# Moving the last 96 columns of w1 into a projection, packing 34-row products in pairs, and fixing the order of a fused attention and MLP kernel by a table

## The chip, the cores and the metric

One NeuronCore of one Trainium2 chip. The metric is the device time of one execution in microseconds. The engines are TensorE (PE), VectorE (DVE), ScalarE (ACT), GpSimd (POOL) and SyncE (SP), which issues the DMAs.

## The reference

One sequence of S = 2048 tokens, D = 512 channels, 32 heads of 16, a hidden width of F = 1376. Attention looks at 8 positions, two tokens apart.

```python
def _A_ref(x, wqkv, wo):              # attention
    qkv = (x @ wqkv) -> q, k, v per head
    idx = pos[:, None] - (arange(8) * 2)[None, :]
    logits = einsum("bhsd,bhswd->bhsw", q, k[idx]) * Dh ** -0.5   # masked where idx < 0
    o = einsum("bhsw,bhswd->bhsd", softmax(logits), v[idx])
    return o.reshape(B, S, D) @ wo
def _B_ref(x, w1, b1, w2, b2):        # MLP
    h = gelu(layernorm(x) @ w1 + b1)
    return h @ w2 + b2
xn = layernorm(x)
return x + _A_ref(xn, wqkv, wo) * silu(_B_ref(xn, w1, b1, w2, b2))
```

## The kernel before

Every product is made of three fp16 products: a number is split into a high and a low fp16 part, and high x high, high x low and low x high are added in PSUM. With D = 512 = 4 x 128 a tile of projections takes 3 x 4 = 12 matmuls.

Tokens are split by parity (c = 0, 1), since the attention steps two tokens at a time, and into 16 tiles of 128. Heads are split into four blocks (hb). This makes eight units u, one for each (c, hb). `qkv(c, hb, u)` multiplies the 8 token tiles of a parity with the 384 columns of q, k and v of the block (L746), scales them on the way out of PSUM (ACT L763, DVE L759) into a buffer `U`, and SP copies shifted rows within `U` (L771), so that a neighbour in time lies on the same partition. `attention(c, hb, u)` then works on DVE:

- four products of 2048 columns q x k (L805), each summed over the head by a reduction (L808);
- the softmax (L828 to L837, with the exponential on ACT at L831);
- four products of 2048 columns of weights, which lie in PSUM (`pl`), with v (L863);
- their sum over the window. The sum of the first two products is one addition of 2048 columns on POOL (L873), the sum of the last two one on DVE (L858); both are then halved by POOL additions of 1024 columns (L883). Each of these comes behind a copy of one element (`gate`, L882), which holds it back until a q x k product of the next unit has ended, so that it runs beside a reduction;
- the high part (ACT L846) and the low part (DVE L848) of the output `o`, then a DMA transpose.

The MLP runs between these in four chunks (ch) of 512 tokens and 11 blocks (f) of 128 hidden columns; the last block has 96. `mlp1(ch, f)` makes the hidden columns (L1016), ACT applies gelu and writes the high part (L1036), DVE writes the low part from PSUM (L1038). `mlp2(ch, f)` adds a block to the four output tiles `z` (L1052). The last block of mlp2 has 96 hidden rows and one for the bias: 97. Output products are L929 and L961; DVE (L993, L1000) and POOL (L997) join the gate and x, and SP stores.

In the head, weights are loaded in fp32, ACT sums their squares for a scale (L514 for wqkv, L421 for w1), and ACT and DVE split them into high and low parts (L536, L543; L482, L486). The first tiles of y are cast by ACT (L687) after a transpose on PE.

The order is made in Python when the program is built. `Plan.add` records each operation with what it reads and writes, a priority and a duration; `Plan.issue` repeatedly takes, from the operations whose predecessors are placed, the one that can start earliest by a model of the engines (of equal ones the one with the first priority), and writes the instructions in that order. Each engine runs its own instructions strictly in the order in which they were written.

Of the kernel before, what the change touches and what calls it, by code (L numbers as in the profile page):

```python
# [8 lines left out]
F32 = mybir.dt.float32  # L9
F16 = mybir.dt.float16  # L10
# [23 lines left out]
LASTPOOL = (0, 2, 4)  # L34

# [3 lines left out]
LAG = 2  # L39

# [28 lines left out]
BEFORE_W1 = (0, 1, 4, 5)  # L69

# [26 lines left out]
class Plan:  # L97
# [89 lines left out]
    def place(self, o, t):  # L187

        if o.eng == "sp":
            if not o.nbytes:  # L190
                return t
            self.free["sp"] = t + o.issue
            self.dma = max(self.dma, t + o.issue + 0.3)
            self.dma += o.nbytes / (o.rate if self.dma > SLOW else 265e3)
            end = self.dma + o.tail
            self.landed.append((end, o.nbytes))
            return end
# [24 lines left out]
    def issue(self):  # L222
# [5 lines left out]
        order = []  # L228
        while len(order) < len(self.ops):
            best = None  # L230
            for e, cand in engs.items():
# [95 lines left out]
def tile_mixer(ctx, tc, a_x, a_xt, a_wqkv, a_wo, b_w1, b_b1, b_w2, out):  # L327
# [34 lines left out]
    ident = sb.tile([P, P], F32, name="ident")  # L362
    make_identity(nc, ident)
    fours = sb.tile([P, 2 * P], BF16, name="fours")
    nc.vector.memset(fours, 4.0)
    mean1 = sb.tile([P, P], F32, name="mean1")
    nc.vector.memset(mean1, 1.0 / D)
    halves = sb.tile([P, 16], F32, name="halves")
# [3 lines left out]
    misc = sb.tile([P, 512], F32, name="misc")  # L372
    v0 = misc[64:65]


    wq = sb.tile([P, NHB, 2, KT, 384], F16, name="wq")
    w1 = sb.tile([P, 2, KT * F], F16, name="w1")
# [6 lines left out]
    b1T = sb.tile([P, NF], F32, name="b1T")  # L384
    hlast = sb.tile([P, 2, 512], F16, name="hlast")
# [7 lines left out]
    R_mx = Ring(sb, [P, 64], F32, 4, "mx")  # L393
    R_cs = Ring(sb, [P, NI], F32, 8, "cs")
# [72 lines left out]
    def low_pool(n, lo, get, s, hi, **k):  # L467
# [4 lines left out]
        pool(0.45 + n * 3.9e-3, fn, **k)  # L472
# [36 lines left out]
    def scale_q(hb):  # L509
        col = R_s.new()  # L510
        for k in range(0, KT, 2):
            def go(k=k):
                src = stq[hb]()[:, k * 384:(k + 2) * 384]
                nc.scalar.activation(wq[:, hb, 0, k:k + 2].bitcast(BF16),  # L514
# [11 lines left out]
    def prep_q(hb):  # L526
# [3 lines left out]
        for k in range(0, KT, st):  # L530
            n = st * 384
            dst = [wq[:, hb, t, k:k + st].rearrange("p k e -> p (k e)") for t in range(2)]
            src = lambda k=k, n=n: stq[hb]()[:, k * 384:k * 384 + n]
# [117 lines left out]
    def y0(i):  # L651
# [12 lines left out]
        elif Y_ENG[i] == "pool":  # L664
            pool(1.25, lambda: nc.gpsimd.tensor_scalar(x(), x(), mv0[:, q, 0:1], rb0[:, q:q + 1], op0=ALU.subtract,
# [54 lines left out]

    def qkv(c, hb, u):
# [13 lines left out]
        raw = pl.users([("xc", j) for j in FP]) if u == 1 else set()  # L735
        csk = {i: (cs, g) for g in parts for i in g} if u == 0 else {i: cs for i in range(NI)}
        for n, i in enumerate((IORD0, IORD1)[u] if u < 2 else IORD):
# [5 lines left out]
            def mm(n0=0, n1=12, y=y, o=o, b=b):  # L743
                for n in range(n0, n1):
                    (s, t), k = ((0, 0), (1, 0), (0, 1))[n // KT], n % KT
                    nc.tensor.matmul(b.t[:, 0:384], y[:, s, k, o:o + P], wq[:, hb, t, k],  # L746
# [5 lines left out]
            for n0, n1 in zip([0] + ends, ends):  # L752
                pe(n1 - n0, 384, lambda mm=mm, n0=n0, n1=n1: mm(n0, n1), [("yh" if n1 <= 4 else "y", c, i)] +
# [8 lines left out]
            else:  # L762
                act(384, lambda i=i, b=b: nc.scalar.activation(  # L763
                    U3[:, i:i + 31:15, :], b.t[:, 0:384].rearrange("p (t e) -> p t e", t=3),
                    AF.Identity, scale=cs.t[:, cp(i):cp(i) + 1]), **ev)

# [241 lines left out]
    def mlp1(ch, f):  # L1008
        M = P if f < NF - 1 else FL
# [15 lines left out]
        if f < NF - 1:  # L1025
            h = R_h.new()
            hi, lo = (lambda: h.t[:, 0]), (lambda: h.t[:, 1])
        else:
            h = ("hlast",)
            hi, lo = (lambda: hlast[:, 0]), (lambda: hlast[:, 1])  # L1030
        hk = (h, 0) if f < NF - 1 else ("hlast", 0)
# [9 lines left out]
        hq[f] = (hi, lo, M if f < NF - 1 else M + 1, h, hk)  # L1041

    def mlp2(ch, f):
        hi, lo, K, h, hk = hq.pop(f)
        for t in range(4):
# [3 lines left out]
            def mm(t=t, z=zt[t]):  # L1049
                hl = (hi(), lo())  # L1050
                for n, (s, w) in enumerate(((0, 0), (0, 1), (1, 0))):
                    nc.tensor.matmul(z.t, hl[s][0:K, t * P:(t + 1) * P], w2[0:K, w, f],  # L1052
                                     start=(f == 0 and n == 0), stop=(f == NF - 1 and n == 2))
            pe(3, 512, mm, [h, hk, w2key[f]] + ([("hrow",)] if f == NF - 1 else []), [zt[t]])
# [23 lines left out]
    def mlp(n):  # L1078
        for _ in range(n):
# [4 lines left out]
            if p < len(steps):  # L1084
# [20 lines left out]
    def zero_halo(b):  # L1105
# [7 lines left out]
          lambda: f32v(s1h.t, 1)[:, 0, 0:W1C[4] - W1C[3]]]  # L1113
    s1k = [[("s1a", n, 0)] for n in range(2)] + [[s1o], [s1h]]
    s2a, s2b = f32v(yT[2], 4), f32v(yT[3], 4)
    s2c = [R_f.new() for k in range(3)]
# [250 lines left out]
```

## Time and profile before

| what | value |
|---|---|
| median of 3 runs | 414.9 us (414.75 to 414.92) |
| the profiled execution's own time | 415.18 us |
| its span in the trace | 413.4 us |
| PE busy | 405.9 us (98%) |
| DVE busy | 379.5 us (92%) |
| ACT busy | 222.1 us (54%) |
| POOL busy | 120.3 us (29%) |
| granted clock | 0.999 |

The profile is of one execution; its times count from the start of the span. An engine can be busy nearly all the time without being the bound, and the chain that ended last says which one was followed back from the end. In the lists of groups a row gives line, engine, operation, out<-in, shape and count, then busy time and the mean in ns of one, then the idle time before.

### The profile page before, as it was taken

The page shows a single profiled execution, that of the slowest core. Times are in us where ns is not written, and L with a number is a line of the kernel's source. Part 1 is how long each engine was busy: PE and PEld are TensorE (multiplying, and loading weights), DVE is VectorE, ACT ScalarE, POOL GpSimd, SP SyncE. Part 2 cuts the span into 40 slices and gives each one's busy share as a digit, 9 for nine tenths or more (in the row PEclk, how much of TensorE's full clock was granted, in tenths as well). Part 3 has the DMA queues.
Part 4 walks back from the last instruction along what each step waited for, and adds up shares of the span by engine and source line. Part 5 has one row for each costly group of instructions (what it writes and reads, how often), then busy time and mean ns, then how long its engine had stood idle before and what let it go on. Part 6 is the DMA issues. An engine that isn't in the chain of part 4 may idle for free.

```text
span 413.4 us, 5554 instructions
## 1 busy us (share of the span) xinstructions
PE 405.9 (98%) x2083; PEld 206.6 (50%) x2083; DVE 379.5 (92%) x379; ACT 222.1 (54%) x353; POOL 120.3 (29%) x131
## 2 busy tenths in 40 slices
PE   8799999999999999999999999999999999999996
PEld 5555544445654455445544554455455544444443
DVE  4996989998999999989998999999999998999954
ACT  4699899994549655843384252225212393263500
POOL 3834002004380425042504330434033404520021
PEclk9999999999999999999999999999999999999999
DMA  8958717030045137720172034223604244007133
GB/s 281 397 112 258 235 61 230 0 128 1 1 142 152 28 93 183 149 46 2 48 221 75 0 102 116 68 86 88 205 7 122 88 111 145 0 18 238 23 102 131
DMA packets 47211, 46.41 MB, mean 112 GB/s; under 512 B 31785, under 2 KB 32225, under 8 KB 46673
## 3 DMA queue, kind: packets, MB, share of 16 engines
q1 hardware_dynamic: 47184, 46.06, 37.6%
q8 instruction: 16, 0.26, 0.3%
q14 instruction: 11, 0.08, 0.1%
HBM read 24.06 MB, written 7.34 MB: 76 GB/s over the span
## 4 chain that ended last, share of the span: by engine, by line
PE 92%; ACT 3%; issue 1%; DVE 1%; POOL 1%; ACTq 0%
PE z L1052 28%; PE ps L1016 28%; PE ps L746 25%; PE ps L929 5%; PE ps L961 2%; PE z L961 2%; PE pl L746 1%; ACT w L421 1%; PE pl L961 1%; ACT f L673 1%; ACT yT L687 0%; ACT wq L536 0%; POOL wq L471 0%; POOL rb L635 0%; ACT prod L661 0%
## 5 line engine op out<-in xcount | busy, mean ns | idle before, releaser
L1016 PE MATMUL ps<-yT,w 128*128 128x512 f16 (+1 forms) x528 | 120.4, 379 | 0.0
L746 PE MATMUL ps<-wq,yT 128*128 128x384 f16 x708 | 117.0, 326 | 0.2 <-DVE U L759 0.2
L1052 PE MATMUL z<-w,h 128*128 128x512 f16 x480 | 110.4, 379 | 0.0
L746 PEld LDWEIGHTS <-yT 128*128 128x128 f16 x744 | 72.5, 98 | 49.2 <-issue 1.0
L1016 PEld LDWEIGHTS <-w 128*128 128x128 f16 (+1 forms) x528 | 52.8, 100 | 61.0
L805 DVE TENSOR_TENSOR prod<-U 128x2048 f32<-128x2048 f32 x32 | 73.2, 2286 | 2.2 <-POOL prod L883 0.7
L1052 PEld LDWEIGHTS <-h 128*128 128x128 f16 x480 | 46.6, 98 | 55.5 <-issue 0.3
L808 DVE TENSOR_REDUCE L<-prod 128x128 f32<-128x2048 f32 x32 | 73.0, 2281 | 0.4
L1033 ACT ACTIVATE ps<-ps,b1T,hsc 128x512 f32<-128x512 f32 (+1 forms) x44 | 32.9, 748 | 73.4 <-PE ps L1016 72.2
L863 DVE TENSOR_TENSOR prod<-pl,U 128x2048 f32<-128x2048 f32 x28 | 63.2, 2283 | 4.2 <-POOL prod L873 4.1
L763 ACT ACTIVATE U<-ps,cs 128x384 f32<-128x384 f32 x54 | 31.2, 580 | 65.2 <-PE ps L746 65.2
L873 POOL TENSOR_TENSOR prod<-prod,prod 128x2048 f32<-128x2048 f32 x7 | 31.7, 4531 | 113.8 <-DVE prod L863 99.6
L883 POOL TENSOR_TENSOR prod<-prod 128x1024 f32<-128x1024 f32 x14 | 32.9, 2349 | 0.0
L882 POOL COPY gate<-prod 1x1 f32<-1x1 f32 x21 | 5.5, 264 | 91.0 <-DVE prod L805 82.2
L1038 DVE SCALAR_TENSOR_TENSOR h<-ps,hsc,h 128x512 f16<-128x512 f32 x40 | 29.6, 741 | 1.7 <-ACT h L1036 1.4
L1036 ACT ACTIVATE h<-ps,hsc 128x512 f16<-128x512 f32 x40 | 27.3, 684 | 1.3 <-PE z L1052 0.4
L929 PE MATMUL ps<-wo,oT 128*128 128x512 f16 x96 | 21.7, 379 | 0.0
L858 DVE TENSOR_TENSOR prod<-prod,prod 128x2048 f32<-128x2048 f32 x9 | 20.5, 2282 | 0.0
L1033 ACT ACT_TABLE_LOAD x10 | 12.8, 1283 | 8.6 <-PE ps L1016 8.5
L883 POOL TENSOR_TENSOR prod<-prod,prod 128x1024 f32<-128x1024 f32 x7 | 16.4, 2347 | 0.0
L961 PEld LDWEIGHTS <-oT 128*128 128x128 f16 x108 | 10.6, 98 | 10.4
L929 PEld LDWEIGHTS <-oT 128*128 128x128 f16 x96 | 9.4, 98 | 11.2
(179 smaller groups left out, 377.8 us busy)
## 6 DMA issues: line engine op xcount, KB each, us to landing
f<-in_A_x_dram SPq DMA_DIRECT2D x31, 256.0 KB, 3.5
U<-U SPq DMA_DIRECT2D x16, 392.0 KB, 4.0
gd<-f SPq DMA_DIRECT2D x12, 256.0 KB, 3.4
prod<-in_A_x_dram SPq DMA_DIRECT2D x8, 256.0 KB, 6.9
oT<-in_B_w_dram SPq DMA_DIRECT2D x2, 1024.0 KB
yT<-in_B_w_dram SPq DMA_DIRECT2D x2, 1024.0 KB, 7.9
f<-gd SPq DMA_DIRECT2D x8, 256.0 KB, 2.7
out_dram<-f SPq DMA_DIRECT2D x8, 256.0 KB, 2.8
```

Source lines behind the costliest of these rows:

```text
L746: nc.tensor.matmul(b.t[:, 0:384], y[:, s, k, o:o + P], wq[:, hb, t, k], start=(n == 0), stop=(n == 11))
L763: act(384, lambda i=i, b=b: nc.scalar.activation(U3[:, i:i + 31:15, :], b.t[:, 0:384].rearrange("p (t e) -> p t e", t=3), AF.Identity, sca ...
L805: dve(2048, lambda p2=p2, g=g: nc.vector.tensor_tensor(p2(), q, slots(Ut, KH, 2 * g), op=ALU.mult), qk + [("kh", ub, 0), ("kh", ub, 1), (" ...
L808: dve(2048, lambda pr=pr, g=g: nc.vector.tensor_reduce(L3()[:, 2 * g:2 * g + 2], pr.t.rearrange("p (r f d) -> p r f d", r=2, d=DH), AX.X, ...
L863: dve(2048, lambda: nc.vector.tensor_tensor(pr.t.rearrange("p (r f d) -> p r f d", r=2, d=DH), A3()[:, 2 * g:2 * g + 2].rearrange("p r (f ...
L873: pool(4.75, lambda: nc.gpsimd.tensor_tensor(acc.t, acc.t, p1.t, op=ALU.add), [acc, p1], [acc])
L883: nc.gpsimd.tensor_tensor(x.t[:, 0:1024], x.t[:, 0:1024], y(), op=ALU.add)
L929: nc.tensor.matmul(b.t, oT[:, hb, i // 4, s, i % 4], wo[:, t, hb], start=(hb == 0 and n == 0), stop=(hb == last and n == 2))
L961: nc.tensor.matmul(b.t[:, cols], oT[:, hb, i // 4, s, i % 4], wo[:, t, hb, cols], start=(start and hb == 0 and n == 0), stop=(stop and hb ...
L1016: nc.tensor.matmul(b.t[0:M], w1[:, s, f * 512 + k * M:f * 512 + (k + 1) * M], yT[ch][:, t, k], start=(n == 0), stop=(n == 11))
L1033: act(512, lambda: nc.scalar.activation(b.t[0:M], b.t[0:M], AF.Gelu_apprx_tanh, bias=b1T[0:M, f:f + 1], scale=hsc[0:M, 1:2]), [b, ("b1T",) ...
L1052: nc.tensor.matmul(z.t, hl[s][0:K, t * P:(t + 1) * P], w2[0:K, w, f], start=(f == 0 and n == 0), stop=(f == NF - 1 and n == 2))
```

## The change

The last 96 columns of w1 are stored behind the 384 columns of `wq[2]`. The tiles of that head block are 480 columns wide (L864), and the 48 products of mlp1's last block are gone. For each such tile ACT writes the 96 columns to a buffer, with tokens on partitions; `last_block` adds the bias on POOL (L817), applies gelu and makes the high parts on ACT, the low parts on DVE (L827), and transposes them by DMA.

In `mlp2` the last block's three parts of 96 rows, 288 in all, and two rows for the bias are packed as two full products of 128 rows for each output tile (L1172) and one of 34 rows (L1175). Two of the 34-row products, for two output tiles, stand at partitions 0 and 64.

A table ORDER of all operations replaces the choice in `issue`. The lines of the operations move: L805 is L930 after, L808 L933, L863 L988, L873 L998, L848 L973, L858 L983, L1038 L1159, L746 L864, L1016 L1141, L961 L1086, L421 L504, L536 L619, L514 L597, L687 L770, L713 L796, L920 L1045, L486 L569, L543 L626.

```diff
+ORDER = (
+    0, 1, 2, 3, 4, 5, 6, 7, 110, 130, 118, 122, 116, 114, 111, 117, 129, 113, 115, 19, 240, 121, 120, 20, 21,
...
-        order = []
+        order, fixed = [], [self.ops[n] for n in reversed(ORDER)]
         while len(order) < len(self.ops):
             best = None
-            for e, cand in engs.items():
+            if fixed:
+                o = fixed.pop()
+                t = max([self.earliest(o)] + [min(b.ring.free) for b in o.bufs if b.slot is None])
+                best = (t, o)
+            for e, cand in engs.items() if best is None else ():
...
+    def last_block(ch):
...
+            pool(1.0, lambda: nc.gpsimd.tensor_tensor(x3(), x3(), row, op=ALU.add), xk + [("b1T",)], xk)
+            act(n, lambda: nc.scalar.activation(x, x, AF.Gelu_apprx_tanh), xk, xk,
...
     def qkv(c, hb, u):
+        wide = 384 + FL * (hb == HLAST)
...
-                    nc.tensor.matmul(b.t[:, 0:384], y[:, s, k, o:o + P], wq[:, hb, t, k],
+                    nc.tensor.matmul(b.t[:, 0:wide], y[:, s, k, o:o + P], wq[hb][:, t, k],
...
+            if hb == HLAST:
+                act(FL, lambda i=i, b=b: nc.scalar.activation(
+                    hpt[i // 4][:, (i % 4) * FL:(i % 4 + 1) * FL], b.t[:, 384:384 + FL], AF.Identity, scale=hsc[:, 1:2]),
...
     def mlp2(ch, f):
+        for a in range(0, 4, 2) if f == NF - 1 else ():
+            def pair(a=a, z=list(zt)):
+                ha = hlt[ch % 2].rearrange("p a (t x) -> p (a t) x", t=4)
+                for t in range(a, a + 2):
+                    for w in range(2):
+                        nc.tensor.matmul(z[t].t, ha[:, 2 * t + w], w2[:, w, f], start=False, stop=False)
+                for t in range(a, a + 2):
+                    r = slice(64 * (t - a), 64 * (t - a) + FR + 2)
+                    nc.tensor.matmul(z[t].t, hlc[ch % 2][r, a // 2], w2t[r], start=False, stop=True)
...
-            if p < len(steps):
+            if p < len(steps) and steps[p][1] < NF - 1:
```

Some buffers are shared or shorter (rings `mx` 4 to 2, `cs` 8 to 7), and two more pieces of w2 are loaded.

What the table does to the instructions is seen on three engines. ACT's first instructions before, where `wq` is written from staged wqkv and `w_79` from staged w1 (`o_105`, `h_106`):

```order
L514 ACTIVATE wq,s_122<-prod_93 128x768 x2
L536 ACTIVATE wq<-prod_93,qsc 128x384 x4
L514 ACTIVATE wq,s_124<-U_87 128x768
L687 CAST yT_82<-z_146 128x4x128
L514 ACTIVATE wq,s_124<-U_87 128x768
L659 ACTIVATE rb_151<-pb_150,rb_151 128x1
```

And after, where the staged pieces of w1 are `h_113` (load w3) and `o_112` (load w2):

```order
L597 ACTIVATE wq_82,s_126<-prod_100 128x768 x2
L597 ACTIVATE wq_83,s_127<-U_94 128x768
L619 ACTIVATE wq_82<-prod_100,qsc 128x384 x3
L504 ACTIVATE wq_84,s_129<-h_113 128x4x96
L504 ACTIVATE w_86,s_129<-o_112 128x1024
L619 ACTIVATE wq_82<-prod_100,qsc 128x384
L597 ACTIVATE wq_83,s_127<-U_94 128x768
L770 CAST yT_89<-z_150 128x4x128
```

The two sums of squares of w1 stood in rows 26 and 27 before; now they stand ahead of the last high part of wq_82, the sum of squares of hb 1 and the first tile's cast.

SP's loads before, from the last piece of wqkv (`U_87`) on; `prod_95` is a tile of x:

```order
L505 DMA U_87<-in_A_wqkv_dram 128x768
L1126 DMA oT<-in_B_w_dram 128x2048
L1126 DMA o_105<-in_B_w_dram 128x1024
L1099 DMA prod_95<-in_A_x_dram 128x512
L1126 DMA h_106<-in_B_w_dram 128x384
L1099 DMA prod_95<-in_A_x_dram 128x512
L1126 DMA oT<-in_B_w_dram 128x2048
```

And after:

```order
L588 DMA U_94<-in_A_wqkv_dram 128x768
L1231 DMA prod_102<-in_A_x_dram 128x512 x2
L1258 DMA oT<-in_B_w_dram 128x2048
L1258 DMA o_112<-in_B_w_dram 128x1024
L1258 DMA h_113<-in_B_w_dram 128x384
```

Both tiles of x moved ahead of the pieces of w1.

DVE in the attention of unit 3 before; the first two L863 are what POOL adds with L873 (`prod_94` and `prod_95`), and the fourth writes `prod_95` again:

```order
L863 TENSOR_TENSOR prod_94<-pl_142,U_87 128x2048
L1038 SCALAR_TENSOR_TENSOR h_107<-ps_140,hsc,h_107 128x512
L863 TENSOR_TENSOR prod_95<-pl_142,U_87 128x2048
L1038 SCALAR_TENSOR_TENSOR h_108<-ps_141,hsc,h_108 128x512
L863 TENSOR_TENSOR prod_93<-pl_142,U_87 128x2048
L1038 SCALAR_TENSOR_TENSOR h_106<-ps_139,hsc,h_106 128x512
L863 TENSOR_TENSOR prod_95<-pl_142,U_87 128x2048
```

And after; POOL's L998 here adds `prod_101` to `prod_102`:

```order
L988 TENSOR_TENSOR prod_101<-pl_146,U_94 128x2048
L988 TENSOR_TENSOR prod_102<-pl_146,U_94 128x2048
L973 SCALAR_TENSOR_TENSOR o_112<-prod_100,osc,o_112 128x2x512
L988 TENSOR_TENSOR prod_101<-pl_146,U_94 128x2048
L1159 SCALAR_TENSOR_TENSOR h_113<-ps_145,hsc,h_113 128x512
L988 TENSOR_TENSOR prod_100<-pl_146,U_94 128x2048
```

The low part of the previous unit's output (L973, which reads `prod_100`) now stands between the products, and the third product writes a buffer that POOL's addition reads.

183 lines of the change are left out of this document (126 added, 57 removed), and 61 rows, old and new, of the table ORDER.

## The prediction

> **What bounds the kernel now.** I read the page first: the busy time of each engine and the chain that ended last.
>
> ```profile
> PE 405.9 (98%) x2083; PEld 206.6 (50%) x2083; DVE 379.5 (92%) x379; ACT 222.1 (54%) x353; POOL 120.3 (29%) x131
> ...
> PE 92%; ACT 3%; issue 1%; DVE 1%; POOL 1%; ACTq 0%
> ```
>
> TensorE (PE) is the bound, but VectorE (DVE) is not far behind it. The windows view over the attention stage, 44 to 394 us, shows how near. Its columns are: stretch, length, then busy time of PE, PEld, DVE, ACT and POOL.
>
> ```profile
> 44.00:394.00 350.00, 349.96 (x1774) 174.05 (x1773) 335.62 (x277) 188.25 (x295) 95.20 (x101) 1.00 0.33 93
> ```
>
> PE never stops in these 350 us, and DVE is idle for only 350.00 - 335.62 = 14.4 us of them. So there are two bounds side by side: what the change saves on PE shows only if DVE does not get longer, and each microsecond that DVE stands still beyond its 14.4 moves the end. The chain in order of time (start, us, what) and DVE's timeline (start, us, engine, line) give the rest of the frame.
>
> ```profile
> 46.38 10.36 PE ps L1016 x48
> ...
> 101.60 15.60 PE ps L746 x96
> ...
> 378.65 2.59 PE ps L1016 x12
> ...
> 396.78 1.94 PE ps L961 x9
> ...
> 409.80 0.49 DVE U L993
> ```
> ```profile
> 43.99 2.28 DVE L805 TENSOR_TENSOR prod<-U 128x2048 f32<-128x2048 f32 x1
> ...
> 392.97 0.75 DVE L848 SCALAR_TENSOR_TENSOR o<-prod,osc,o 128x512 f16<-128x512 f32 x1 [0.79 <-ACT o L846]
> ```
>
> The attention runs on DVE from 43.99 to 393.72; the last output products follow on PE from 396.78. A 384-column matmul costs 15.60/96 = 0.1625 us, a 512-column one 2.59/12 = 0.2158, so a column costs (0.2158 - 0.1625)/128 = 0.000416 us and 96 columns 0.040.
>
> **The products: what the diff is about.** The groups by form hold what goes.
>
> ```profile
> L1052 PE MATMUL z<-w,hlast 97*128 97x512 f16 x48 | 11.0, 379 | 0.0
> L1016 PE MATMUL ps<-yT,w 128*96 128x512 f16 x48 | 11.0, 379 | 0.0
> ```
>
> Both groups of 48 leave: 96 x 0.2158 = 20.7 us. (The 379 ns of one is latency; in the chain 12 take 2.59.) In return 16 tiles x 12 = 192 matmuls of the third block are 96 columns wider, 192 x 0.040 = 7.7; the 16 token tiles get two full products each, 32 x 0.2158 = 6.9; and 8 pairs of 34-row products cost 8 x 0.2158 = 1.7 if the two run at once, 3.5 if one after the other. PE gains 20.7 - 7.7 - 6.9 - 1.7 = 4.4 us (2.7 serially). The trace has no products on half the rows, so a cost of switching is open: none, or at most a full drain at each of 16 switches, 16 x (0.379 - 0.216) = 2.6. I take none, since all other matmuls are issued back to back. The Trainium skill, "TensorEngine Tiling (Array Packing)", section "Key Properties", says that changing the tiling mode drains TensorE; by that rule the 2.6 applies and the gain is 1.8; no run here shows it.
>
> What hangs on it elsewhere is small: 16 evacuations of 96 columns on ACT (54% busy), eight short low parts on DVE in place of four of 0.74, and eight more transposes on SP, all beside PE. The last output tile is 512 wide instead of 256: its two DVE operations take about 0.75 each instead of 0.49, so +0.5 on the end.
>
> **The order, head.** In the new ACT order the sums of squares of w3 and w2 (L504) stand ahead of the fourth low-index cast of wq_82 (L619), of the second half of hb 1 (L597) and of the first tile's cast (L770); before, they came after all of these. And the loads x7 and x6 are now ahead of w0, w2, w3, w1 on SP's queue. The windows of the first stage (last two columns: DMA share, GB/s) and the landing of x7 say when w3 can come.
>
> ```profile
> 10.00:15.00 5.00, 3.35 (x20) 2.40 (x21) 4.78 (x11) 3.30 (x8) 3.25 (x4) 1.00 1.04 413
> 15.00:20.00 5.00, 4.52 (x29) 2.79 (x28) 4.79 (x19) 3.12 (x6) 4.92 (x6) 1.00 1.04 410
> ```
> ```profile
> prod<-in_A_x_dram SPq DMA_DIRECT2D x1, 256.0 KB, 8.2
> ```
> ```profile
> 13.50:31.40 17.90, 17.14 (x101) 10.06 (x100) 17.02 (x46) 15.87 (x30) 10.24 (x10) 1.00 0.73 225
> ```
>
> The queues are full, and the load of x7, issued in the window 9.7 to 10 us, lands 8.2 us later, at 18.0. w3 now stands behind the two tiles of x, 0.5 MB or 1.3 us at 410 GB/s: near 19.3. I take 19.1, as its own 0.2 MB is shorter than a tile of x. ACT must wait for it from about 12. What ACT then does up to the second wq_83 (L619) is what it did in 13.50 to 31.40 before, 15.87 us, and one 384-wide cast of 0.6: done at 35.6 to 36.6. Only then can hb 1's products begin, with 96 of the first 168 still to do; before, (46.38 - 36.0)/0.1625 = 64 were left. PE is 32 x 0.1625 = 5.2 us late. Queued behind ACT's wait is also the last evacuation of unit 0, at about 37.9, and with it the shifted copies of U.
>
> ```profile
> 36.33 3.07 SPq L771 DMA_DIRECT2D U<-U  x4
> ```
>
> Before, the copies were issued at 36.33 and the first L805 could start 7.7 us later. After: 37.9 + 7.7 = 45.6, and up to 48.1 because a 1 MB load (2.5 us at 410 GB/s) now stands between two of the copies. I take 46.5 for the first L930: +2.5 for DVE.
>
> **The order, attention.** POOL adds two 2048-wide products (L873, now L998) in each of seven units while DVE makes the next two. The new order puts other things on DVE beside this add. What that costs is in the timelines.
>
> ```profile
> 136.74 4.55 POOL L873 TENSOR_TENSOR prod<-prod,prod 128x2048 f32<-128x2048 f32 x1 [14.00 <-DVE prod L863]
> ```
> ```profile
> 140.32 1.52 DVE L713 TENSOR_TENSOR f<-f,f 128x512 f16<-128x512 f32 x1
> ...
> 155.06 0.68 DVE L713 TENSOR_TENSOR f<-f,f 128x512 f16<-128x512 f32 x1
> ...
> 261.74 1.82 DVE L920 TENSOR_TENSOR f<-f,f 128x512 f32<-128x512 f32 x1
> ```
> ```profile
> 106.48 1.28 DVE L486 SCALAR_TENSOR_TENSOR wo<-yT,osc,wo 128x1024 f16<-128x1024 f32 x1
> ```
> ```profile
> 106.56 1.24 POOL L882 COPY gate<-prod 1x1 f32<-1x1 f32 x1 [8.88 <-DVE osc L1293]
> ```
>
> L713 reads two operands from SBUF. It takes 0.68 alone, but 1.52 at 140.32: it ended only 0.55 after POOL's add did (141.29). L920 did the same at 261.74 (+1.1). The other way round, a one-element copy on POOL took 1.24 and ended with DVE's L486. So DVE operations with two SBUF operands and POOL's exclude each other; those with a PSUM operand (L863, L1038) run through. The Trainium skill, "SBUF — State Buffer", section "Who interferes with whom", says the same: a DVE instruction with two SBUF inputs contends with a GpSimd instruction that reads SBUF, and whoever issues first blocks the other completely; the trace agrees in these three rows. Two rows speak against so general a rule:
>
> ```profile
> 22.04 0.68 DVE L674 TENSOR_TENSOR f<-prod,f 128x512 f16<-128x512 f32 x1
> ```
> ```profile
> 20.54 2.08 POOL L665 TENSOR_SCALAR prod<-prod,mv,rb 128x512 f32<-128x512 f32 x1
> ```
>
> L674, of L713's kind, took 0.68 though POOL was busy until 22.62. So not each form of POOL locks; the adds do. The prices of the add and of what stands beside it are in the groups by form.
>
> ```profile
> L873 POOL TENSOR_TENSOR prod<-prod,prod 128x2048 f32<-128x2048 f32 x7 | 31.7, 4531 | 113.8 <-DVE prod L863 99.6 <-ACT h L1036 14.2
> ```
> ```profile
> L863 DVE TENSOR_TENSOR prod<-pl,U 128x2048 f32<-128x2048 f32 x28 | 63.2, 2283 | 4.2 <-POOL prod L873 4.1
> L1038 DVE SCALAR_TENSOR_TENSOR h<-ps,hsc,h 128x512 f16<-128x512 f32 x40 | 29.6, 741 | 1.7 <-ACT h L1036 1.4
> ...
> L848 DVE SCALAR_TENSOR_TENSOR o<-prod,osc,o 128x1024 f16<-128x1024 f32 x7 | 9.0, 1281 | 0.6 <-ACT o L846 0.6
> ```
>
> Before, one L863 and two or three L1038 (2.28 + 3 x 0.74 = 4.5) cover POOL's 4.53. After, from the end of the second L988, unit by unit: 0: one L626 first, then 4.3 us of PSUM work, a stall of 0.4. 1: L569, L1159, then L973 (two SBUF operands) blocked, 4.53 - 0.74 = 3.8. 2: L973, L827, L796 exclude the add, and the next L988 needs a buffer that the add reads: the full 4.5. 3: L973, then the same wait: 4.5. 4: 3.8 of PSUM work ahead of L1045: 0.75. 5: L1159, then L827 and L930: 3.8. 6: L1159, then L973: 3.8. Together 21.5 us. Of the same kind before has 4.1 in waits and 0.84 + 1.14 = 2.0 in stretched operations; added: 15.4. Bounds: if only the waits for a buffer counted (units 2, 3 and 5: 2.3 + 3.25 + 3.4 = 9.0), 4.9; if each of seven adds stood bare (31.7 - 6.1), 25.6. I take 15.4, as the blocked rows above are of the same two groups.
>
> Besides, more weight preparation (L569, L626) now lies behind the first L930: over the two orders, at the means of the forms, 3.8 us.
>
> **The sum**, on DVE's path: 413.4 + 2.5 (start) + 3.8 (work) + 15.4 (stalls) - 5 (half of the other 10.3 us of DVE's idle time, which waits for ACT and PE that are early now) - 2 (PE has no other products left under the last transposes) + 0.5 (last tile) = 428.6 us of span. The profiled execution took 415.18 with a span of 413.4, and lies 0.3 above the median of 414.9: 428.6 + 1.8 - 0.3 = 430 us. Nothing of PE's 4.4 shows, since PE then waits for DVE.
>
> **Rivals.**
> - *PE stays the bound* (the stalls at their lower end). On DVE's path 4.9 in place of 15.4 gives 419.6; on PE's path 413.4 + 5.2 - 4.4 + 0.5 + 1.5 = 416.2. So 416 to 420. For it: L674 ran unblocked. Against: L713, L920, the gate copy. Chance 0.18.
> - *Faster.* w3 lands early enough that ACT does not wait, and the stalls fall where DVE would have waited anyhow. Then PE's saving is all there is: 414.9 - 4.4 + 0.5 = 411. The point from which it decides: w3 by about 15.8 rather than 19.1, and no more than some 5 us of stalls. Against: at 410 GB/s the queue moves 1.35 MB in the 3.3 us between, and those loads still stand ahead of it. Chance 0.11, with 0.02 more for a draw.
> - *Both engines in turn.* While DVE stands, PE runs out of low parts (L1159) and of U; then DVE waits for PE's next tiles. If each of the five long stalls costs as much again as half of it, 10 us more: 440 and above. PE's 98% busy time speaks for it, its three buffers of ps against it. Chance 0.07 for over 442.
>
> **How the numbers follow.** DVE's path has 0.62, from 422 to 441 by its bounds. The range 416 to 442 takes in the first rival and leaves out the faster case and the worst. A measurement of this kernel can tell about 0.2% (0.8 us) from no change: faster 0.11, same 0.02, slower 0.87.
>
> **What would show it.** In the profile after: ACT idle from about 12 to 19 us before L504; the first L930 near 46.5; DVE rows L973 or L827 of 4 to 6 us instead of 1.3 or 0.3, and DVE's L988 waiting for POOL's L998 for over 8 us in all; PE's busy time about 401 with some 25 us of idle, its waits naming DVE. I am wrong if PE stays at 98% (then the locks cost little), if L504 of w3 starts before 16 us, or if the pairs take more than 0.5 us each.

## The result, and the profile after

The changed kernel takes **443.62 us** (median of 4 runs, 443.01 to 443.87) against 414.91 us before (414.75 to 415.59 in the runs beside it): a ratio of 1.069, 95% interval 1.067 to 1.071, or 28.7 us more. Forecast were 15.1 us more, with 442.0 as the upper end of the range. So the direction was right and the size was not. The profiled execution has a span of 441.1 us.

The page of the changed kernel: busy time of each engine, and the chain that ended last by engine.

```profile
PE 411.5 (93%) x2035; PEld 201.6 (46%) x2035; DVE 402.8 (91%) x386; ACT 224.7 (51%) x372; POOL 127.4 (29%) x134
...
DVE 39%; PE 13%; issue 8%; POOL 4%; DMA 3%; ACT 1%; SPq 1%; DVEq 0%; ACTq 0%
```

Before, PE was 98% busy and had 92% of the chain. Now it has 13%, and DVE leads. The windows view over the same attention stage (columns as in the prediction) shows PE standing still for 350.00 - 335.22 = 14.8 us, where it had not stopped at all.

```profile
44.00:394.00 350.00, 335.22 (x1656) 160.68 (x1655) 333.68 (x260) 183.60 (x307) 105.26 (x106) 0.99 0.34 90
```

PE's waits (what it waited for: us in all, times, longest) name DVE's low part of the hidden layer, as forecast: PE follows DVE.

```profile
PE z L1184 <- DVE h L1159: 5.9, 4, 3.3
...
PE ps L1141 <- DVE h L1159: 3.0, 2, 2.7
...
PE ps L864 <- DVE h L1159: 1.9, 1, 1.9
```

**The head.** ACT's timeline, with the wait for w3 in brackets, and DVE's, with the first products of the attention and the last low part of o.

```profile
19.14 0.52 ACT L504 ACTIVATE wq<-h 128x384 bf16<-128x384 f32 x1 [7.53 <-DMA h<-in_B_w_dram]
```
```profile
47.88 8.65 DVE L930 TENSOR_TENSOR prod<-U 128x2048 f32<-128x2048 f32 x3 [4.19 <-DMA U<-U]
...
422.78 0.75 DVE L973 SCALAR_TENSOR_TENSOR o<-prod,osc,o 128x512 f16<-128x512 f32 x1 [0.79 <-ACT o L971]
```

w3 lands at 19.14 (forecast 19.1), and ACT stands for 7.5 us before it. The attention begins on DVE at 47.88 instead of 43.99 and ends at 423.53 instead of 393.72.

**The stalls beside POOL's 2048-column add.** These are the rows of DVE in the seven units, in order of time, and two rows of the add itself.

```profile
102.31 2.29 DVE L988 TENSOR_TENSOR prod<-pl,U 128x2048 f32<-128x2048 f32 x1 [0.42 <-POOL prod L998]
...
141.86 4.88 DVE L973 SCALAR_TENSOR_TENSOR o<-prod,osc,o 128x1024 f16<-128x1024 f32 x1
...
186.91 4.73 DVE L827 SCALAR_TENSOR_TENSOR f<-first,hsc,f 128x256 f16<-128x256 f32 x1
...
237.82 2.29 DVE L988 TENSOR_TENSOR prod<-pl,U 128x2048 f32<-128x2048 f32 x1 [4.41 <-POOL prod L998]
...
278.99 1.67 DVE L1045 TENSOR_TENSOR f<-f,f 128x512 f32<-128x512 f32 x1
...
326.40 4.36 DVE L827 SCALAR_TENSOR_TENSOR f<-hl,hsc,f 128x256 f16<-128x256 f32 x1
...
363.03 5.16 DVE L973 SCALAR_TENSOR_TENSOR o<-prod,osc,o 128x1024 f16<-128x1024 f32 x1
```
```profile
140.17 5.49 POOL L998 TENSOR_TENSOR prod<-prod,prod 128x2048 f32<-128x2048 f32 x1 [3.17 <-DVE prod L988]
...
362.60 4.51 POOL L998 TENSOR_TENSOR prod<-prod,prod 128x2048 f32<-128x2048 f32 x1 [10.63 <-DVE prod L988]
```

L973 takes 1.28 us where POOL is idle, L827 about 0.48 and L1045 0.68. Unit by unit the loss is 0.4, 3.6, 4.25, 4.4, 1.0, 3.9 and 3.9: 21.5 us, which is what the prediction walked through (21.5). In unit 6 L973 ends at 368.19, 1.1 us after the add does (367.11): it stood until the add was done.

**What the sum had left out.** More operations with two SBUF operands are stretched, but beside POOL's other work: its 1024-column adds (L1008), a short add (L817), and one subtraction of weights (L554) that stands over the second L930 (the three above took 8.65 us, and three alone take 3 x 2.28 = 6.8).

```profile
109.83 2.52 DVE L569 SCALAR_TENSOR_TENSOR w<-f,zsc,w 128x512 f16<-128x512 f32 x1
...
120.45 2.03 DVE L626 SCALAR_TENSOR_TENSOR wq<-yT,qsc,wq 128x768 f16<-128x768 f32 x1
```
```profile
159.29 1.30 DVE L796 TENSOR_TENSOR f<-f,f 128x512 f16<-128x512 f32 x1
```
```profile
203.33 1.85 DVE L796 TENSOR_TENSOR f<-f,f 128x512 f16<-128x512 f32 x1
```
```profile
109.46 2.34 POOL L1008 TENSOR_TENSOR prod<-prod 128x1024 f32<-128x1024 f32 x1
```

Against the usual time of each form (0.74, 1.01, 0.68, 0.68) these are 1.8, 1.0, 0.6 and 1.2 us; with the 1.9 of L930 and 0.25 of a later L1045, 6.7 in all, where before had 0.3 of the kind.

So DVE's path adds up like this, measured the same way in both traces: 413.4 + 3.9 (start) + 5.3 (work: DVE's busy time between the first product and the last low part of o, without what was stretched, 333.3 to 338.6) + 15.4 (stalls beside the 2048-column add: 21.5 less 6.1 in before) + 6.4 (the other blocked operations) - 1.2 (DVE's other idle time between these two, 10.0 to 8.8) - 2.1 (the end, 19.7 to 17.6) = 441.1, which is the span.

### The profile page after: what moved, and what is told of

The parts are those of the page before. It is cut to its first block, busy times and chain, and to the rows that moved or that the text cites. A ratio compares the mean times of both kernels' runs of the same rounds, so it can differ in the third digit from the quotient of the medians.

```text
span 441.1 us, 5499 instructions
## 1 busy us (share of the span) xinstructions
PE 411.5 (93%) x2035; PEld 201.6 (46%) x2035; DVE 402.8 (91%) x386; ACT 224.7 (51%) x372; POOL 127.4 (29%) x134
## 3 DMA queue, kind: packets, MB, share of 16 engines
q1 hardware_dynamic: 52600, 47.69, 39.4%
## 4 chain that ended last, share of the span: by engine, by line
DVE 39%; PE 13%; issue 8%; POOL 4%; DMA 3%; ACT 1%; SPq 1%; DVEq 0%; ACTq 0%
DVE prod L988 9%; DVE prod L930 8%; DVE L L933 7%; PE z L1184 4%; DVE o L973 3%; DVE h L1159 2%; PE ps L1086 2%; POOL prod L1008 2%; DVE prod L983 2%; PE z L1086 2%; PE ps L864 2%; PE ps L1141 2%; DMA U<-U 1%; DVE f L1068 1%; DVE f L796 1%
## 5 line engine op out<-in xcount | busy, mean ns | idle before, releaser
L864 PE MATMUL ps<-wq,yT 128*128 128x384 f16 (+1 forms) x708 | 132.4, 338 | 3.5 <-DVE h L1159 1.9
L1184 PE MATMUL z<-w,h 128*128 128x512 f16 x480 | 115.5, 381 | 7.1 <-DVE h L1159 5.9
L1141 PE MATMUL ps<-yT,w 128*128 128x512 f16 x480 | 112.1, 383 | 4.2 <-DVE h L1159 3.0
L864 PEld LDWEIGHTS <-yT 128*128 128x128 f16 x744 | 72.9, 98 | 65.5 <-issue 7.0
L930 DVE TENSOR_TENSOR prod<-U 128x2048 f32<-128x2048 f32 x32 | 75.0, 2349 | 6.8 <-DMA U<-U 5.4
L1184 PEld LDWEIGHTS <-h 128*128 128x128 f16 x480 | 46.5, 98 | 62.5 <-DVE h L1159 7.9
L1141 PEld LDWEIGHTS <-w 128*128 128x128 f16 x480 | 46.8, 99 | 61.5 <-issue 8.8
L933 DVE TENSOR_REDUCE L<-prod 128x128 f32<-128x2048 f32 x32 | 72.9, 2282 | 0.4
L988 DVE TENSOR_TENSOR prod<-pl,U 128x2048 f32<-128x2048 f32 x28 | 63.3, 2284 | 5.2 <-POOL prod L998 4.8
L998 POOL TENSOR_TENSOR prod<-prod,prod 128x2048 f32<-128x2048 f32 x7 | 35.2, 5027 | 74.3 <-DVE prod L988 74.3
L1154 ACT ACTIVATE ps<-ps,b1T,hsc 128x512 f32<-128x512 f32 x40 | 29.9, 748 | 42.6 <-PE ps L1141 42.3
L1008 POOL TENSOR_TENSOR prod<-prod 128x1024 f32<-128x1024 f32 x14 | 32.9, 2347 | 0.0
L1159 DVE SCALAR_TENSOR_TENSOR h<-ps,hsc,h 128x512 f16<-128x512 f32 x40 | 29.7, 744 | 1.0 <-ACT h L1157 1.0
L1054 PE MATMUL ps<-wo,oT 128*128 128x512 f16 x96 | 21.5, 379 | 0.0
L983 DVE TENSOR_TENSOR prod<-prod,prod 128x2048 f32<-128x2048 f32 x9 | 20.6, 2290 | 0.2
L971 ACT ACTIVATE o<-prod,osc 128x1024 f16<-128x1024 f32 (+1 forms) x9 | 9.5, 1052 | 21.4 <-DVE prod L983 14.2
L973 DVE SCALAR_TENSOR_TENSOR o<-prod,osc,o 128x1024 f16<-128x1024 f32 (+1 forms) x9 | 17.9, 1991 | 0.8 <-ACT o L971 0.8
L1008 POOL TENSOR_TENSOR prod<-prod,prod 128x1024 f32<-128x1024 f32 x7 | 16.4, 2348 | 0.0
L1086 PEld LDWEIGHTS <-oT 128*128 128x128 f16 x108 | 10.4, 98 | 10.2 <-issue 0.5
```

What stands on the lines that cost most here:

```text
L864: nc.tensor.matmul(b.t[:, 0:wide], y[:, s, k, o:o + P], wq[hb][:, t, k], start=(n == 0), stop=(n == 11))
L930: dve(2048, lambda p2=p2, g=g: nc.vector.tensor_tensor(p2(), q, slots(Ut, KH, 2 * g), op=ALU.mult), qk + [("kh", ub, 0), ("kh", ub, 1), (" ...
L933: dve(2048, lambda pr=pr, g=g: nc.vector.tensor_reduce(L3()[:, 2 * g:2 * g + 2], pr.t.rearrange("p (r f d) -> p r f d", r=2, d=DH), AX.X, ...
L973: dve(n, lambda: nc.vector.scalar_tensor_tensor(o16.t[:, h0:h1, 1], o2(), osc[:, 1:2], o16.t[:, h0:h1, 0], op0=ALU.mult, op1=ALU.subtract) ...
L988: dve(2048, lambda: nc.vector.tensor_tensor(pr.t.rearrange("p (r f d) -> p r f d", r=2, d=DH), A3()[:, 2 * g:2 * g + 2].rearrange("p r (f ...
L998: pool(4.75, lambda: nc.gpsimd.tensor_tensor(acc.t, acc.t, p1.t, op=ALU.add), [acc, p1], [acc])
```

## The experiments

The kernels with an edited table number their lines 6 higher (L973 is L979 there, L988 L994, L998 L1004, L1159 L1165): their loop takes the first entry of the table that can be placed, and no longer simply the next one. The kernels without a table have their own numbers, given at their place. Before ran beside every batch, at 414.7 to 415.1 us.

**1. The order alone (e1_planner).** All of the change but the table; the order comes from the priorities, as in before.

```diff
-ORDER = (
...
-)
+ORDER = ()
```

> The changed kernel with an empty table: the choice by priorities and durations makes the order, as before the change; products, buffers and loads stay as changed. If the order alone costs the time (theory: DVE stands under POOL's additions, and ACT waits for w3 in the head), the time is near what the products give, 414.9 - 4.4 + 1.6 for the switches of the pairs as the trace of the changed kernel has them (about 0.2 us each) + 0.5: 411 to 414 us. If the changed products are themselves the cause (rival: wider tiles, their evacuations on ACT, the bias on POOL and the transposes), it stays above 430.

Measured: 421.73 us (1.016, 1.013 to 1.018). So 21.9 of the 28.7 us are the table's order, and 6.8 stay that it does not explain; neither theory had these (run 12 wins most of them back with other priorities). In this kernel PE is the bound again (96% busy), and what is lost is on PE. PE's timeline (L1121 is the second product here, L502 and L506 the casts of its weights), then windows across it, the clock being the third number from the end:

```profile
66.95 0.58 PE L1121 MATMUL z<-w,h 128*128 128x512 f16 x1 [4.34 <-ACT w L502]
...
69.29 1.01 PE L1121 MATMUL z<-w,h 128*128 128x512 f16 x2 [1.75 <-DVE w L506]
```
```profile
60.00:62.00 2.00, 2.00 (x11) 0.88 (x9) 2.00 (x2) 1.88 (x5) 0.00 (x0) 1.00 0.00 0
...
68.00:70.00 2.00, 0.71 (x2) 0.26 (x2) 2.00 (x3) 2.00 (x3) 0.00 (x0) 0.50 0.00 0
70.00:72.00 2.00, 2.00 (x6) 0.76 (x5) 2.00 (x3) 1.97 (x5) 0.66 (x1) 0.50 0.72 214
72.00:74.00 2.00, 2.00 (x8) 0.71 (x6) 1.85 (x3) 0.85 (x2) 1.92 (x2) 0.60 0.81 266
74.00:76.00 2.00, 2.00 (x11) 0.94 (x10) 1.53 (x3) 2.00 (x5) 0.85 (x1) 1.00 1.04 340
```

PE stands for 6.1 us for weights, and then runs until about 74 at half its clock: 6 matmuls in 2 us instead of 11. These gaps on PE are paid about 1.4 times: 6.1 us, and some 2.3 more for what runs slowly behind them. The Trainium skill, "TensorE: Matmul & The Clock Gate", Part 1, says that an idle PE falls to half its clock and comes back after some 3.4 us of steady work; these rows agree (PE works on from 69.29, and 0.60 between 72 and 74 puts the full clock's return near 73.6, 4.3 us later).

**2. The units cleared (e2_clear).** In all seven units the operations with two SBUF operands are moved away from the add, and in the table of units 1 to 6 low parts L1159 are pulled forward from behind, where there are fewer than three, to stand beside it. An entry that cannot be placed yet is passed over, so that in the trace each of these six units has one low part there. The rows of DVE in unit 6, old and new order:

```diff
+L973 SCALAR_TENSOR_TENSOR o<-prod,osc,o
 L988 TENSOR_TENSOR prod<-pl,U x2
+L988 TENSOR_TENSOR prod<-pl,U
 L1159 SCALAR_TENSOR_TENSOR h<-ps,hsc,h
-L973 SCALAR_TENSOR_TENSOR o<-prod,osc,o
-L1045 TENSOR_TENSOR f<-f,f
-L988 TENSOR_TENSOR prod<-pl,U
-L1045 TENSOR_TENSOR f<-f,f
 L988 TENSOR_TENSOR prod<-pl,U
```

> The changed kernel with the table edited at seven places only: in each unit the low part of the previous output goes ahead of the products with v, other operations with two SBUF operands go behind them, and low parts from PSUM come between the third and the fourth product. Theory of the additions: the stalls beside L998 fall from 21.7 us to about 8.5 (six waits of 1.3 to 1.7), so 13 us off: 430 us, with 428 to 434. Rival, that DVE only follows a PE that has become late: 440 to 444, the same time spent in other waits.

Measured: 470.15 us (1.133, 1.129 to 1.137), far above either expectation. No operation of DVE is blocked by the 2048-column add any more, and the waits for its buffer are 4.3 us in all, but DVE's waits read:

```profile
DVE h L1165 <- ACT h L1163: 37.8, 11, 6.9
```

A low part needs the hidden layer's high part from ACT, which needs PE's product. Pulled forward, it makes DVE wait, and PE then waits for DVE. This is the rival "both engines in turn", made by hand.

**3. The head alone (e3_head).** The sums of squares of w3 and w2 (entries 180, 179) go behind that of the other half of w1 (178), and a cast of hb 1's weights (175) goes ahead of them.

```diff
-49, 47, 41, 45, 180, 179, 43, 169, 68,
+49, 47, 41, 45, 43, 169, 68,
...
-140, 93, 173, 177, 178, 60, 97,
+140, 93, 173, 175, 177, 178, 180, 179, 60, 97,
...
-95, 96, 182, 99, 175, 183, 153,
+95, 96, 182, 99, 183, 153,
```

> The changed kernel with the table edited in the head only: on ACT the sums of squares of w3 and w2 come behind those of the other pieces of w1, and the second half of hb 1's high part comes ahead of all of them. Theory: ACT's wait of 7.5 us goes, the first L930 starts 4 to 6 us earlier (at 42 to 44 in place of 47.9), and since DVE's path sets the end, the time falls by the same 4 to 6: 437 to 440. Rival, that the head is swallowed later on: within 1 us of 443.6.

Measured: 440.43 us (1.061, 1.058 to 1.063), 3.2 us less than the changed kernel. The first L930 moves from 47.88 to 45.63, 2.2 us where 4 to 6 were expected, and the spans of the two profiled executions differ by 2.0. The start is a term of its own, and smaller than expected.

**4. The add taken away (e4_noadd).**

```diff
-            pool(4.75, lambda: nc.gpsimd.tensor_tensor(acc.t, acc.t, p1.t, op=ALU.add), [acc, p1], [acc])
+            pool(4.75, lambda: nc.gpsimd.tensor_tensor(acc.t[:, 0:1], acc.t[:, 0:1], p1.t[:, 0:1], op=ALU.add), [acc, p1], [acc])
```

> The changed kernel with POOL's addition of 2048 columns cut to one column, in the same place of the order and with the same semaphores; it leaves out the sum of the first two products. Theory: with nothing of length on POOL there, both the blocked operations and the waits for a buffer go, 21.7 us in all, and 421 to 424 us are left. Rival, that what blocks is not POOL (ACT's high parts or the transposes come late at the same places): the stalls stay, above 435.

Measured: 428.35 us (1.032, 1.030 to 1.033), 15.3 us less where 20 to 23 were expected. All 21.5 us of stalls are gone, but behind its first product DVE now waits 6.0 us for the copies of U (1.2 in the changed kernel), which follow PE's tiles; why not all of the time is won, runs 6 and 7 say.

**5. Writes instead of an add (e5_memset).**

```diff
-            pool(4.75, lambda: nc.gpsimd.tensor_tensor(acc.t, acc.t, p1.t, op=ALU.add), [acc, p1], [acc])
+            pool(4.75, lambda: [nc.gpsimd.memset(acc.t[:, 0:n], 0.0) for n in (2048, 2048, 768)], [acc, p1], [acc])
```

> The changed kernel with GpSimd's 2048-column add in a unit (L998) replaced by three fills of the same buffer (2048, 2048 and 768 columns, meant to last about as long), in the same place of the order; the sum of the first two products is left out. The fills write SBUF and read nothing. If VectorE's two-input operations are held by anything that GpSimd runs there, the rows beside it stay as they are: L973 4.9 and 5.2 us (plain 1.28), L827 4.4 to 4.7 us (plain 0.5), and the time stays at 440 to 444 us. If they are held only while GpSimd reads two SBUF inputs, those rows fall to 1.3 and 0.5 us and the time comes to 426 to 430 us, as with the add cut to one column (428.35).

Measured: 427.93 us (1.030, 1.025 to 1.036). POOL's and DVE's timelines in unit 1:

```profile
137.15 4.47 POOL L998 MEMSET prod<- 128x2048 f32 x3 [3.15 <-DVE prod L988]
```
```profile
138.86 1.27 DVE L973 SCALAR_TENSOR_TENSOR o<-prod,osc,o 128x1024 f16<-128x1024 f32 x1
140.17 2.29 DVE L988 TENSOR_TENSOR prod<-pl,U 128x2048 f32<-128x2048 f32 x1
```

POOL is busy just as long (4.47 us) and holds the same buffer, and L973 takes 1.27 us in the midst of it. So what holds DVE back is an operation of POOL that reads SBUF, not its being busy and not the order as such. The Trainium skill, "SBUF — State Buffer", section "Who interferes with whom", says that a DVE instruction with two SBUF inputs contends with a GpSimd instruction that reads SBUF and not with one that only writes it; this run shows the second half too.

**6. The other adds as well (e9_noadds).**

```diff
-                        nc.gpsimd.tensor_tensor(x.t[:, 0:1024], x.t[:, 0:1024], y(), op=ALU.add)
+                        nc.gpsimd.tensor_tensor(x.t[:, 0:1], x.t[:, 0:1], y()[:, 0:1], op=ALU.add)
```

The line of run 4 is changed too.

> The changed kernel with both kinds of GpSimd adds in a unit cut to one column: the 2048-column add (L998) and the three 1024-column adds (L1008); these sums are left out. Against the run with the 2048-column add cut alone (428.35 us) three blocked operations of VectorE beside L1008 remain to go: L569 +1.8, L796 +1.0, L1045 +0.25, together 3.0 us. If each blocked operation counts in full, as the missed term of the sum has it: 425 to 426 us. If they stand over other waits: 428 us.

Measured: 428.29 us (1.033, 1.031 to 1.035), the same as run 4. DVE's stretched time falls by 3.6 us more (6.9 to 3.3), and that buys nothing here. Its windows say why:

```profile
150.00:200.00 50.00, 50.00 (x263) 25.56 (x262) 48.08 (x37) 26.12 (x43) 3.81 (x16) 1.00 0.44 105
200.00:250.00 50.00, 50.00 (x263) 25.24 (x262) 47.02 (x32) 23.67 (x37) 3.49 (x21) 1.00 0.40 89
```

PE is busy for all of it, as it was before the change. Freed of the stalls, DVE has slack and PE is the bound. All of PE's gaps over 0.3 us lie before 62.5 us: 11.6 us against 3.2 in before, the last of them 2.7 us long. So 428 is about what the table's order costs on PE.

**7. The same adds, with the stalls left standing (e13_no1024).** Only the line of run 6 is changed; the 2048-column add stays.

> The changed kernel with GpSimd's three 1024-column adds of a unit (L1008) cut to one column, the 2048-column add left whole; the sums of these three adds are left out. In the changed kernel four VectorE operations beside L1008 are blocked: L569 +1.8, L626 +1.0, L796 +1.2, L1045 +0.25, together 4.2 us, a part of the 6.7 us that the prediction's sum had left out. If they lengthen VectorE's path one for one as long as the stalls beside the 2048-column add stand: 439 to 440 us (changed kernel 443.62). If they stand over waits that come anyway, as with both kinds of adds cut: 442 to 444 us.

Measured: 439.76 us (437.14 to 441.19; 1.059, 1.055 to 1.062), 3.9 us less than the changed kernel. The runs lie 4 us apart, so the gain is known only as some 2 to 6 us: the 4.2 of one for one fits, and nothing at all does not. Where DVE is the path, the stretched operations beside the smaller adds belong in the sum.

**8. Head and add together (e12_noadd_head).** The edits of runs 3 and 4.

> The changed kernel with GpSimd's 2048-column add cut to one column (its sum left out; 428.35 us) and the edit of the table's head (440.43 us alone, 3.2 us under the changed kernel). With the add cut, TensorE has no gap over 0.3 us after 62.5 us. If VectorE still set the pace there and the two terms of the prediction's sum were independent: 425 us. If TensorE is the bound by then, only what the head saves of TensorE's gaps counts (10.0 us of gaps up to 62 us in the head-alone run against 11.3 us with the add cut alone): 426.5 to 428 us.

Measured: 425.31 us (1.025, 1.023 to 1.026), 3.0 us under run 4, so the head is worth as much here, where PE has no gap over 0.3 us after 59 us and is the bound. It is not the gaps: they fall only from 11.3 to 10.7 us, while PE's busy time falls from 407.6 to 404.7. In the profiled executions the head runs at another clock, run 4's first:

```profile
11.00:18.00 7.00, 6.43 (x20) 3.86 (x19) 5.09 (x16) 0.58 (x2) 3.91 (x4) 0.52 1.05 415
```
```profile
11.00:18.00 7.00, 5.34 (x30) 3.38 (x29) 5.72 (x17) 3.21 (x8) 4.51 (x4) 1.00 1.05 415
```

The clock need not be all of it: executions of the two kernels with the same mean clock, 0.985, still differ (425.7 against 428.3 and 428.4). The expectation by gaps alone (426.5 to 428) was too simple, and how the head reaches the end in this kernel stays open.

**9. Only the operations moved (e7_mini).** As in run 2, but no low part is pulled forward: in each unit those that the add blocks go ahead of the first product or behind the last add. In unit 6:

```diff
+L973 SCALAR_TENSOR_TENSOR o<-prod,osc,o
 L988 TENSOR_TENSOR prod<-pl,U x2
 L1159 SCALAR_TENSOR_TENSOR h<-ps,hsc,h
-L973 SCALAR_TENSOR_TENSOR o<-prod,osc,o
-L1045 TENSOR_TENSOR f<-f,f
 L988 TENSOR_TENSOR prod<-pl,U
-L1045 TENSOR_TENSOR f<-f,f
 L988 TENSOR_TENSOR prod<-pl,U
```

> The changed kernel with its order table edited at the units alone: the two-input VectorE operations that stand beside GpSimd's 2048-column add are put ahead of the unit's first product or behind the unit's last add (L973 in units 1 and 6, L827 in 2 and 5, L1045 in 4, two evacuating casts in 0), in unit 5 the pair for GpSimd comes first, and the low parts L1159 keep their places as far as they can. Theory (the stalls are lost time one for one, 21.7 us, of which 5 to 6 stand over waits for U that come next anyway): 426 to 430 us. If moving these operations only opens waits elsewhere, as moving the low parts did: 437 us or more.

Measured: 447.14 us (443.60 to 450.21; 1.078, 1.070 to 1.085): nothing won, against an expected 426 to 430. DVE's timeline in unit 6, then its waits:

```profile
367.54 2.29 DVE L994 TENSOR_TENSOR prod<-pl,U 128x2048 f32<-128x2048 f32 x1
371.67 2.29 DVE L994 TENSOR_TENSOR prod<-pl,U 128x2048 f32<-128x2048 f32 x1 [1.85 <-POOL prod L1004]
...
383.33 0.75 DVE L1165 SCALAR_TENSOR_TENSOR h<-ps,hsc,h 128x512 f16<-128x512 f32 x1 [3.64 <-ACT h L1163]
```
```profile
DVE prod L994 <- POOL prod L1004: 11.6, 7, 2.5
...
DVE h L1165 <- ACT h L1163: 5.3, 5, 3.6
```

There are three product buffers, so the fourth product waits until the add has read its second one. Of the add's 4.5 us one product covers 2.3 and, where there is one, a low part 0.7; the rest is now an open wait. DVE's stretched time falls from 23.4 to 8.9 us over the attention, and its idle time rises from 13.6 to 33.0. Some 6.7 us of this rise are waits for the add's buffer (4.8 to 11.6), the stall under another name. The others are longer waits for the copies of U (by 4.8 us) and for ACT's high parts of h and of o (by 4.1 and 3.2). This profile is of the slowest of the four executions.

**10. The same, with the head (e8_minihead).** The edits of runs 3 and 9.

> The same edits of the units, and the edit of the head as in the head-alone run (third and second MLP weight casts behind the other sums of squares; -3.2 us there). If head and units are independent terms of one path on VectorE: 3 us under the units-alone run of this batch. If that start is swallowed by a later wait: the same time as that run.

Measured: 440.98 us (1.063, 1.061 to 1.064), 6.2 us under run 9, whose own runs lie 6.6 us apart, and no better than the head alone (440.43). It agrees with run 9: with the head mended, moving the blocked operations is worth nothing.

**11. Loads first (e10_load).** No table; the loads of the second product's weights go ahead of the second group of U copies.

```diff
-            load(kind, i, [("y", 0, j) for j in BYDMA])
+            with prio(1.0 if kind == "c" and i > 2 else 0.95):
+                load(kind, i, [("y", 0, j) for j in ((4,) if kind == "c" and i > 2 else BYDMA)])
```

> The changed kernel without the order table (order by priorities, 421.73 us before), with one thing moved: the loads of the second product's weights get a priority ahead of the second group of U copies, and the two loads of its last rows wait for one normalized tile instead of four. Without the table TensorE stands still after 62 us only for these weights: 4.3 us for the cast L502 and 1.8 us for L506 at 67 to 69 us, and its granted clock is 0.93 from 48 to 100 us (some 3.6 us of 52). Theory (in that order TensorE is the bound, and what is lost against before is these gaps and the clock that falls with them): 411 to 415 us and a clock of 1.00 in that stretch. If VectorE's work is what the changed weights lengthen there, or the U copies that now come later: 418 to 423 us.

Measured: 420.73 us (1.014, 1.012 to 1.015). The window that was at fault is mended, PE full and its clock back at 1.00; but a new gap stands later.

```profile
48.00:100.00 52.00, 51.98 (x248) 23.52 (x246) 51.24 (x59) 46.72 (x92) 6.37 (x9) 1.00 0.37 120
```
```profile
141.50 1.86 PE L1121 MATMUL z<-w,h 128*128 128x512 f16 x4 [2.46 <-ACT f L1137]
```

The forecast of 411 to 415 fell: one gap was moved, and 1.0 of some 7 us came back, which is hardly clear of noise between two batches.

**12. Three priorities more (e11_prio).**

```diff
-PU0 = 0.8687
+PU0 = 0.6643
...
-PS1 = 1.1561
+PS1 = 0.8258
...
-            with prio(1.0 if kind == "c" and i > 2 else 0.95):
+            with prio(0.85):
```

> As the run above, with three priorities more: those loads at 0.85 (1.0 there without the edit), the first unit's products at 0.6643 instead of 0.8687, the sums of squares of the first product's weights at 0.8258 instead of 1.1561. A try for a version that beats both kernels. If TensorE is the bound and only gaps before 70 us are to be won: 411 to 415 us. If the reordered head delays the first unit on VectorE: 418 us or more.

Measured: 416.38 us (1.0034, 1.0022 to 1.0047): 27 us better than the changed kernel, and still some 1.6 us behind before. It is the best version of the change, and did not beat the kernel before. It has no PE gap over 0.3 us after 28.2 us, and a clock of 1.00 from the start to 400 us, so here the products can be priced beside before's. Groups by form, before first:

```profile
L746 PE MATMUL ps<-wq,yT 128*128 128x384 f16 x708 | 117.0, 326 | 0.2 <-DVE U L759 0.2
```
```profile
L801 PE MATMUL ps<-wq,yT 128*128 128x480 f16 x192 | 39.4, 366 | 0.0
...
L1109 PE MATMUL z<-w,hl 128*128 128x512 f16 x16 | 4.1, 380 | 0.0
L1109 PE MATMUL z<-w,first 128*128 128x512 f16 x16 | 4.1, 380 | 0.0
L1112 PE MATMUL z<-tail 34*128 34x512 f16 x16 | 3.1, 386 | 0.0
```

The two groups of 48 that left had 22.0 us. In their place stand 39.4 - 192 x 117.0/708 = 7.7 for the wider block, 8.2 for the full products and 3.1 for the eight pairs: 19.0. The change saves PE 3.0 us. But the gaps in the head are 6.0 us against 3.2, and PE's busy time in all falls from 405.9 to 404.3 only, so its other groups take 1.4 more. That is 1.2 us more than the 3.0 saved, as the spans have it (414.6 against 413.4).

```profile
PE 404.3 (98%) x2035; PEld 199.1 (48%) x2035; DVE 380.0 (92%) x386; ACT 230.4 (56%) x375; POOL 126.5 (31%) x134
```

## Why the prediction was right and wrong

**Right, and to the size.** The engine that sets the end changes from PE to DVE. w3 lands at 19.14 (19.1). The stalls beside the 2048-column add are 21.5 us (21.5), in the units and at the operations named, though unit 2 shows its loss as a blocked L827 and not as a wait, so that L988 waits for L998 only 4.8 us in all, where over 8 were named. The end is 2.1 shorter (1.5).

**Wrong: "- 5 (half of the other 10.3 us of DVE's idle time ...)".** That idle time went only from 10.0 to 8.8 us. The step took for granted that DVE, once late, finds ACT and PE early. In both traces 4.7 us of it are gaps of under 0.3 us between instructions, which DVE's lateness did not take back. This term was chosen, not read from a row. It cost 3.8 us of the forecast.

**Wrong: the sum priced the exclusion at one operation of POOL only.** The prediction said that two-operand operations and POOL's adds exclude each other, and then walked only through L998. L1008, L817 and L554 on POOL block L569, L626, L796 and an L930 in the same way, 6.4 us net, which the sum had at nothing; run 7 took 3.9 us back by cutting the 1024-column adds. The upper end of the range, 442, left them out as well, and 443.62 lies above it.

**Too small: the start and the work.** "I take 46.5" was 47.88, near the 48.1 that the text gave as the upper end: 1.4 us. SP issued the two groups of copies at 38.60 and 39.90, one load of w2 between them, and the first L930 came 9.3 us behind the first group, where the forecast had 7.7 behind 37.9 and a part of the load. The work behind the first L930 rises by 5.3 instead of 3.8, 1.5 more.

Together: 3.8 + 6.4 + 1.4 + 1.5 (work) - 0.6 (end) = 12.5 of the 12.5 us between the forecast span of 428.6 and 441.1. Why L674 ran unblocked beside L665 in the kernel before, the row that the prediction quotes against the rule, no run tests.

**The pairs.** The forecast took switching as free and gave half a microsecond as the point at which it would be wrong. A pair costs 0.42 us by its starts (0.312 + 0.003 + 0.318 - 0.216; by busy time 3.1/8 = 0.39), not 0.216, and PE gains 3.0 us instead of 4.4. The bound of a full drain (2.6 for 16 switches) was too high and the value taken, none, too low. As forecast, nothing of it shows in the time.

**The rivals.** "PE stays the bound, 416 to 420" is what the change is without its table (421.73, and 416.38 at best): the right account of the products, and the wrong one of the order. That 416.38 meets its 416.2 is luck: this sum has a head that is 5.2 us late, and the gaps of run 12's head are only 2.8 us longer than before's. "Both engines in turn" gave 440 and above, and the time did end there, but by another mechanism: DVE's idle time did not grow (14.1 to 13.6 us). That mechanism showed itself when run 2 moved the low parts. "PE's busy time about 401" came out as 411.5. Run 12, with the same products and the full clock, has 404.3; in the changed kernel the granted clock is 0.50 for 17.0 us before the last tiles (11.6 to 18.4, 21.8 to 25.2, 62.8 to 66.2 and 199.3 to 202.7).

**What fell on the way.** After the result I held that the stalls were time lost one for one, to be had back by moving the blocked operations. Runs 2, 9 and 10 refute the second part. Run 5 lets the same operations run in the same places, and the time falls by 15.7 us; moving them out leaves the add uncovered and opens waits for U and ACT. What the order before has, and the table lost, is work with a PSUM operand at hand when the add runs. That three buffers alone make the fourth product wait is read from the timeline; a fourth buffer was not tried.

## What to carry to other kernels

Where two engines share a lock, price every pair of instructions that meets across it, not the longest alone, and let no idle time pay for it unless a row shows what would fill that. A blocked operation is also cover: before moving it away, ask what will stand in its place until the other engine is done. And on an engine that never stops, a gap of some 2.5 us or more can cost more than its length, by the clock behind it.

## What the runs showed of the hardware

- A VectorE operation with two SBUF operands stands until GpSimd's add is done (5.16 us instead of 1.28), and runs at its usual 1.27 us beside fills of the same length.
- Two 34-row products on different halves of the array start 3 to 4 ns apart. The first begins 0.31 us after the full product ahead of it, instead of 0.216, and the next full product 0.32 us after the second: about 0.1 us into the mode and 0.1 us out of it.
- A gap of 2.7 us in TensorE's work (60.16 to 62.82 us in the changed kernel) can be enough for the granted clock to fall to 0.50 for some 3 us behind it (the first four windows, of the changed kernel). The length alone does not decide: a gap of 3.32 us before 199.95 is followed by 0.50 in the changed kernel, and one of 3.33 before 196.70 in run 7 by no fall at all (the row and the last window). The changed kernel's gaps of 1.1 to 1.9 us (before 165.8, 269.1, 294.1 and 371.6) are not followed by any fall either.

```profile
60.00:62.00 2.00, 0.16 (x1) 0.00 (x0) 2.00 (x2) 0.17 (x1) 0.00 (x0) 1.00 0.00 0
62.00:64.00 2.00, 1.18 (x3) 0.41 (x3) 1.90 (x9) 0.56 (x1) 0.00 (x0) 0.69 0.00 0
64.00:66.00 2.00, 2.00 (x6) 0.76 (x5) 1.89 (x3) 2.00 (x4) 0.00 (x0) 0.50 0.00 0
66.00:68.00 2.00, 2.00 (x10) 0.87 (x9) 2.00 (x2) 2.00 (x3) 0.00 (x0) 0.95 0.47 61
```
```profile
196.70 1.04 PE L1184 MATMUL z<-w,h 128*128 128x512 f16 x4 [3.33 <-DVE h L1159]
```
```profile
190.00:210.00 20.00, 16.67 (x89) 8.50 (x88) 19.79 (x14) 7.41 (x14) 0.32 (x2) 1.00 0.55 113
```
